# The first expert's output layer in float32, the output weights split during the second expert

## The chip, the cores and the metric

The kernel runs on one core of a Trainium2 chip. The metric is the device time of one launch in microseconds (us); lower is better.

## What is computed

Three layers follow each other: banded attention, a mixture of eight experts in which each token goes to one expert with at most 288 tokens each, and a gated unit. The reference, cut:

```python
B, H, S, D = 4, 8, 576, 64            # attention: a window of 128 keys, a slope per head
attn_out = softmax(scale * q @ k.T + bias, masked) @ v
x = attn_out.transpose(0, 2, 1, 3).reshape(2304, 512)

logits = x @ w_gate                   # 2304 tokens, 8 experts, cap = 288
for idx in np.argsort(-logits.flatten()):      # best pair first
    tok, e = idx // 8, idx % 8
    if assigned[tok] < 0 and counts[e] < cap:
        assigned[tok] = e; counts[e] += 1
x[mask] = np.maximum(x[mask] @ w1[e], 0) @ w2[e]          # per expert, 512 -> 1024 -> 512

g, val = x @ m2_gate, x @ m2_val      # 512 -> 1536, all tokens
out = (g / (1 + exp(-g)) * val) @ m2_out                  # 1536 -> 512
```

## The kernel before

**Stages.** The attention runs first, until about 135 us. Then eight experts follow, one after the other. For each, a routing finds which expert fills up next and the list of its tokens; the tokens are gathered from memory (`xg`), turned on TensorE into `X` with tokens as columns, and taken through all that is left: the first expert layer (8 products, tile `P` used as hidden rows), the second (4 products, `O`), the gate and value layer of the gated unit (12 pairs of products with the weights `GV`), and the output layer with the weights `WO`, whose rows are scattered to the output.

**Precision.** TensorE works on 16-bit pairs: a value is split into a high and a low half, and a product takes three passes (`layer`, L1066). ScalarE makes the high half, VectorE the low one. The first expert alone (`first`, L1103) has its two expert layers in float32 (`layer32`, L1074), so that its weights need no split.

**The gated unit's weights** come as 64-bit integers in 36 chunks, 24 for `GV` and 12 for `WO`, and are turned into float32 on the chip (`glu_weights`, L307). Per chunk VectorE does `shift` (L319, into `cvu`), `join` (L323, into `cvt`), `carry` (L331) and `low` (L346); ScalarE does the lower word (`cvr`) and the high half, both through L293. Most of this runs beside the first expert.

**The first expert's output layer** (`results`, L1177) has two row groups of 128 tokens, c0 and c1, of 12 steps of the inner sum each. For this expert alone they are taken in the order of the weights' arrival: four steps of c0, four of c1, and so on. The other 32 tokens are gathered into `PR` for a later expert. What feeds the layer is `z` (L1146, silu times value), its high half (L1150, ScalarE) and its low half (L1153, VectorE).

**What sets the order.** `Plan` (L120) orders all work before anything runs: each step has an engine, an estimated length and a due time, and a greedy pass takes steps by due time and estimated start. Each engine then runs its own list strictly in order, with waits between engines. `RINGS` gives the number of buffers of each tile, `ROUTE` the due times of the routings relative to the expert's. The second expert's routing (`route`, L717) is a chain of small steps that goes back and forth between VectorE and TensorE while the first expert computes: it ends with the expert's number (`eid`, L813), the choice (`sg`, L818 to L820), places (L840 to L864), a one-hot array (`oc`, L867), 18 small products that list the tokens (L872) and the list itself (`idx`, L877 to L880). Only then can the gather (L1017, GpSimd) start. The expert's weights are loaded through SyncE (L970) into `stw`, three buffers, once `eid` is known, and split by ScalarE (L973) and VectorE (L977) into `WE`.

Of the kernel before, what the change touches and what calls it, by code (L numbers as in the profile page):

```python
# [31 lines left out]
    "stg": 3, "cvt": 4, "cvr": 2, "cvu": 1,  # L32
# [10 lines left out]
ROUTE = ((20, 66), (-5, 30))  # L43
WA = 7
TA, TN = (12, 22), (1.5, 2.5)
GD = (14, 50)
LATE = 1.6
# [72 lines left out]
class Plan:  # L120
# [41 lines left out]
    def ported(self, t, engine):  # L162

        return engine == "Pool" or (engine == "DVE" and t["port"])
# [23 lines left out]
    def run(self, fit, need=None):  # L188
# [5 lines left out]
        while left:  # L194
# [10 lines left out]
            for e, c in by.items():  # L205
# [3 lines left out]
                fits = [x for x in c if x[2] + x[3] <= first[2] + fit]  # L209
# [46 lines left out]
def body(ctx, tc, a, out):  # L256
# [46 lines left out]
    WO = []  # L303
    stage = ctx.enter_context(tc.tile_pool(name="stage", bufs=RINGS["stg"]))
    cv = ctx.enter_context(tc.tile_pool(name="cv", bufs=1))

    def glu_weights(c, due):  # L307
# [9 lines left out]
        def shift(e):  # L317
            v["u"] = cv.tile([128, 512], I32, name="cvu", bufs=RINGS["cvu"])
            nc.vector.tensor_scalar(v["u"], v["f"][:, :, 1], 3, 0x3FFFFFF8, op0=OP.logical_shift_left, op1=OP.bitwise_and)  # L319

        def join(e):
            v["t"] = cv.tile([128, 512], I32, name="cvt", bufs=RINGS["cvt"])
            nc.vector.scalar_tensor_tensor(v["t"], v["f"][:, :, 1], -0x40000000, v["u"], op0=OP.bitwise_and,  # L323
                                           op1=OP.bitwise_or)
# [4 lines left out]

        def carry(e):  # L330
            nc.vector.tensor_add(v["t"], v["t"], v["r"])  # L331

        def parts():
            if c < 24:
                return [GV[:, c % 2, m, c // 2] for m in range(2)]
            d, k = divmod(c - 24, 3)
            return [WO[0][:, m, 4 * k:4 * k + 4, d * 128:d * 128 + 128] for m in range(2)]

        def flat(t):
            return t if c < 24 else t.rearrange("p (k c) -> p k c", k=4)  # L340

        def high(e):
            copy_scaled("ACT", parts()[0], flat(v["t"].bitcast(F32)), SG)

        def low(e):
            nc.vector.scalar_tensor_tensor(parts()[1], flat(v["t"].bitcast(F32)), SG, parts()[0], op0=OP.mult, op1=OP.subtract)  # L346

        add("DMA", dma(2 ** 19), due, fetch, w=[("stg", c)], late=LATE)
        add("DVE", dve(512, 2), due, shift, r=[("stg", c)], w=[("cvu", c)], port=True)
        add("DVE", dve(512), due, join, r=[("stg", c), ("cvu", c)], w=[("cvt", c)], port=True)  # L350
        add("ACT", act(512), due, lower, r=[("stg", c)], w=[("cvr", c)])
        add("DVE", 0.66, due, carry, r=[("cvr", c)], w=[("cvt", c)], port=True)
# [589 lines left out]

    WO.append(big.tile([128, 2, 12, DM], F16, name="WO"))

# [62 lines left out]
    def tokens(k, u):  # L1007
# [13 lines left out]
        for c in range(3):  # L1021
            add("Pool", 1.03, u - ta, lambda e, c=c: fetch(e, c),
                r=[("idx", k)] + [("x_dram", b, kt) for b in range(B) for kt in range(5)], w=[("xg", k, c)])
# [58 lines left out]
    def expert(k, u):  # L1082
# [47 lines left out]
        for f in range(12):  # L1130
            v = {}
            for m in range(2):
# [10 lines left out]
                else:  # L1143
# [4 lines left out]

                    def high(e, f=f, v=v):
                        nc.scalar.activation(P()[:, 0, f], v["z"], AF.Copy)  # L1150
# [3 lines left out]

                    add("DVE", dve(CAP), u, value, r=[key, ("tt", (k, f))], w=[("z", (k, f))])
# [7 lines left out]
        def gather_rest(e):  # L1163
            if ("PR", g) not in T:
                T["PR", g] = wk.tile([128, 2, 12, 128], F16, name="PR", bufs=RINGS["PR"])
            if e == "ACT":
                nc.scalar.activation(T["PR", g][:, :, :, r], P()[:, :, :, 256:CAP], AF.Copy)
            else:
                nc.vector.tensor_copy(T["PR", g][:, :, :, r], P()[:, :, :, 256:CAP])

        add({"ACT": act(768), "DVE": dve(768)}, None, u, gather_rest, r=[y for f in range(12) for y in both("P", (k, "P"), f)],
            w=[("PR", g, k % 4)])
        pieces = {3: (0, 1, 2), 7: (0, 2, 1)}.get(k, (0, 1))
        for c in pieces:
            v = {}

            def results(e, a, c=c):  # L1177
# [3 lines left out]
                for kk in range(4 * a, 4 * a + 4):  # L1181
# [101 lines left out]
```

## Time and profile before

| | |
|---|---|
| Median of 3 runs | 874.05 us (873.32 to 874.25) |
| The profiled execution | 875.06 us |
| Its span, first to last instruction | 873.3 us |
| TensorE busy | 819.2 us, 94% of the span |
| VectorE busy | 507.9 us, 58% |
| ScalarE busy | 343.5 us, 39% |
| Share of the chain that ended last | TensorE 73%, VectorE 10%, waiting for nothing shown 10%, DMA 3% |

A share of the span is a mean over stages with different limits; the page's rows in 40 slices show VectorE at 80 to 90% of each slice from the second to the twelfth (22 to 262 us) and mostly well below that afterwards, while TensorE is full nearly everywhere except in slices 7 and 8 (131 to 175 us) and slices 12 and 13 (240 to 284 us). A stage is read from the timelines: which engine waits, and for whom. A wait stands in square brackets behind the row that ended it.

### The profile page before, as it was taken

Reading aid. Unit: us, or ns where it says so; the run is one execution under the profiler, and the core shown is the slowest. Engines: PE = TensorE matmul, PEld = TensorE weight load, DVE = VectorE, ACT = ScalarE, POOL = GpSimd, SP = SyncE. Lnnn points to the kernel's source line nnn. Section 1 sums busy time; section 2 is a strip of 40 time slices with the busy share of each in tenths; the row PEclk is TensorE's granted clock in tenths of the full one; section 3 lists DMA queues with packets and bytes.
Section 4 is the critical chain, followed back from the end, with each engine's and each line's share of the span. In section 5 each row is a group of like instructions: output and inputs, shape, how many; then the busy total and the mean of one; then the engine's idle time right before and its main releaser. Section 6 shows DMA issues by size and latency. Waiting matters only on the chain.

```text
span 873.3 us, 16974 instructions
## 1 busy us (share of the span) xinstructions
PE 819.2 (94%) x6666; PEld 589.5 (68%) x6666; DVE 507.9 (58%) x1585; ACT 343.5 (39%) x774; POOL 136.5 (16%) x195
## 2 busy tenths in 40 slices
PE   7999994699965999999999999999999999999997
PEld 6887883377732678577757764777577667757763
DVE  3888889889995648445833671367337735312220
ACT  5788882255543314312521341135113434212220
POOL 5586761100002001000100011001000020000001
PEclk9999996599986999999999999999999999999999
DMA  8798523754536004201400240024002532000000
GB/s 274 300 322 300 182 68 91 271 196 162 157 112 220 25 1 151 85 10 66 153 28 2 81 141 36 3 73 149 25 1 100 170 116 81 2 13 13 2 1 36
DMA packets 32064, 92.05 MB, mean 105 GB/s; under 512 B 3952, under 2 KB 10480, under 8 KB 31216
## 3 DMA queue, kind: packets, MB, share of 16 engines
q1 hardware_dynamic: 29008, 81.53, 27.8%
q0 software_dynamic: 2976, 9.44, 3.2%
q8 instruction: 52, 0.85, 0.4%
q14 instruction: 28, 0.23, 0.1%
HBM read 81.52 MB, written 9.44 MB: 104 GB/s over the span
## 4 chain that ended last, share of the span: by engine, by line
PE 73%; issue 10%; DVE 10%; DMA 3%; ACT 2%; POOL 1%; SPq 0%; POOLq 0%; DVEq 0%; ACTq 0%
PE mm L1071 45%; PE mm L1183 13%; PE mm L1077 3%; PE s L535 3%; PE mm L1040 2%; PE o L595 2%; PE t L555 2%; DVE cvt L331 1%; DVE cvt L323 1%; DMA x_dram<-xr 1%; PE rp L872 1%; PE rp L765 1%; DVE tl L570 1%; DVE sc L543 1%; DVE WO L346 1%
## 5 line engine op out<-in xcount | busy, mean ns | idle before, releaser
L1071 PE MATMUL mm<-O,GV 128*128 128x288 f16 x2304 | 292.0, 286 | 0.0
L1071 PEld LDWEIGHTS <-GV 128*128 128x128 f16 x2304 | 220.8, 98 | 55.7
L1071 PEld LDWEIGHTS <-WE 128*128 128x128 f16 x1344 | 128.1, 98 | 34.7 <-issue 1.6
L1183 PE MATMUL mm<-WO,P 128*128 128x512 f16 x576 | 131.2, 385 | 0.0
L1183 PEld LDWEIGHTS <-P 128*128 128x128 f16 x576 | 55.5, 99 | 65.4 <-issue 3.3
L1150 ACT ACTIVATE P<-z 128x288 f16<-128x288 f32 x96 | 42.3, 441 | 120.1 <-DVE z L1146 118.3
L1071 PE MATMUL mm<-X,WE 128*128 128x288 f16 x672 | 89.2, 290 | 0.0
L1071 PE MATMUL mm<-P,WE 128*128 128x288 f16 x672 | 86.1, 286 | 0.0
L977 DVE SCALAR_TENSOR_TENSOR WE<-stw,WE 128x512 f16<-128x512 f32 x112 | 74.0, 684 | 4.6 <-ACT WE L973 4.4
L1192 POOL DMA_INDIRECT out_dram<-R,idx x16 | 16.0, 999 | 381.9 <-ACT R L1188 362.3
L1146 DVE SCALAR_TENSOR_TENSOR z<-mm,t 128x288 f32<-128x288 f32 x96 | 43.6, 454 | 48.7 <-PE mm L1071 48.1
L1017 POOL DMA_INDIRECT xg<-x_dram,idx x24 | 24.9, 1037 | 290.7 <-issue 204.6
L973 ACT ACTIVATE WE<-stw 128x1024 f16<-128x1024 f32 x56 | 58.3, 1051 | 18.0 <-DMA stw<-in_w_dram 17.9
L535 PE MATMUL s<-kt,qb 128*128 128x192 f32 (+2 forms) x288 | 58.2, 336 | 4.6 <-DMA kt<-in_kT_dram 4.6
L1153 DVE TENSOR_TENSOR P<-z,P 128x288 f16<-128x288 f32 x96 | 43.9, 457 | 28.8 <-ACT P L1150 26.6
L549 ACT ACTIVATE pb<-sc,mx 128x192 f32<-128x192 f32 (+2 forms) x144 | 56.0, 431 | 10.6 <-DVE mx L543 10.4
L1140 ACT ACTIVATE t<-mm 128x288 f32<-128x288 f32 x96 | 39.2, 409 | 47.7 <-PE mm L1071 43.7
L535 PEld LDWEIGHTS s<-kt,qb 128*128 128x128 f32 x288 | 46.6, 203 | 6.7 <-DMA qb<-in_qB_dram 4.0
L1000 DVE SCALAR_TENSOR_TENSOR P<-mm,P 128x288 f16<-128x288 f32 x56 | 25.5, 455 | 43.1 <-ACT P L995 41.4
L543 DVE CUSTOM_DVE_ANT_0 sc<-s,bias 128x192 f32<-128x192 f32 (+2 forms) x144 | 41.7, 330 | 13.4 <-PE s L535 11.4
L995 ACT ACTIVATE P<-mm 128x288 f16<-128x288 f32 x56 | 23.0, 410 | 63.2 <-PE mm L1071 62.9
L555 PE MATMUL t<-cst,pb 128*128 128x128 f32 x256 | 43.1, 286 | 2.3 <-ACT pb L549 1.9
(141 smaller groups left out, 1002.0 us busy)
## 6 DMA issues: line engine op xcount, KB each, us to landing
stw<-in_w_dram SPq DMA_DIRECT2D x56, 512.0 KB, 3.7
stg<-in_glu_dram SPq DMA_DIRECT2D x36, 512.0 KB, 3.7
qb<-in_qB_dram SPq DMA_DIRECT2D x3, 2304.0 KB, 13.3
x_dram<-xr SPq DMA_DIRECT2D x16, 256.0 KB, 4.1
WE<-in_w_dram SPq DMA_DIRECT2D x8, 512.0 KB, 5.2
kt<-in_kT_dram SPq DMA_DIRECT2D x3, 1152.0 KB, 8.6
vf<-in_vN_dram SPq DMA_DIRECT2D x8, 256.0 KB, 4.4
vt<-in_vT_dram SPq DMA_DIRECT2D x4, 512.0 KB, 7.8
```

The lines of the kernel that those rows point to most:

```text
L535: nc.tensor.matmul(v["s"][:, par, c:], QB[b % 2][:, hp * 9 + i], KT[b % 2][:, hp, (i - 2) * 64 + c:(i + 1) * 64], start=True, stop=True)
L543: nc.vector.tensor_tensor_reduce(out=v["sc"][:, par, c:], in0=v["s"][:, par, c:], in1=bias[:, hp, c:], scale=-0.125, scalar=3.0e38, op0=OP ...
L549: nc.scalar.activation(PB[n % NPB][:, par, 64 * par + c:64 * par + W], v["sc"][:, par, c:], AF.Exp, bias=v["mx"][:, par:par + 1], scale=-1.0)
L555: nc.tensor.transpose(v["t"][:, j, :, par, :], PB[n % NPB][:, par, j * 128:j * 128 + 128], ident)
L973: nc.scalar.activation(WE[:, c, 0], v["f"], AF.Copy, scale=sc)
L977: nc.vector.scalar_tensor_tensor(WE[:, c, 1, at], f[:, at], sc, WE[:, c, 0, at], op0=OP.mult, op1=OP.subtract)
L1071: nc.tensor.matmul(p[:, :at.stop - at.start], w(i, k), x[:, j, k, at], start=(m == 0), stop=(m == 3 * nk - 1))
L1140: nc.scalar.activation(v["t"], T["mm", k, ("gv", f, 0)][:, :CAP], AF.Silu, scale=1.0 / (SO * SG))
L1146: nc.vector.scalar_tensor_tensor(v["z"], T["mm", k, ("gv", f, 1)][:, :CAP], SPR / (SO * SG), v["t"], op0=OP.mult, op1=OP.mult)
L1150: nc.scalar.activation(P()[:, 0, f], v["z"], AF.Copy)
L1153: nc.vector.tensor_sub(P()[:, 1, f], v["z"], P()[:, 0, f])
L1183: nc.tensor.matmul(T["mm", k, "y", c], x[:, i, kk, at], WO[0][:, j, kk, :], start=(kk == 0 and i == j), stop=(kk == 11 and i == 1))
```

## The change

**Weights.** A `WO` chunk ends with `carry`, which now writes float32 straight into `WO`'s place (`WOF`, a float32 view). Its high and low halves are made later by a new function, `split_output_weights`, due during the second expert: per step of the inner sum ScalarE copies the float32 row to a `stg` buffer and writes the high half, VectorE the low half: 24 ScalarE and 12 VectorE instructions.

**The first expert.** `single_value` writes silu times value as float32 into `P`, in place of `z` and its two halves. The output layer takes these and the float32 weights: 24 float32 products in place of 72 16-bit ones. The 32 left tokens are split by one ScalarE and one VectorE instruction (`rest_high`, `rest_low`).

**Chunks.** `shift` writes into the chunk's own `cvt`; `cvu` is gone and `cvt` has 5 buffers. The planner has a new number, `NEAR`: in its last pass it may let VectorE take a step that can start earlier though another is due up to 1.6 us before it. The first `ROUTE` pair moves by 8 us. GpSimd's DMA issues no longer hold the planner's port between VectorE and GpSimd.

```diff
-    "stg": 3, "cvt": 4, "cvr": 2, "cvu": 1,
+    "stg": 3, "cvt": 5, "cvr": 2,
-ROUTE = ((20, 66), (-5, 30))
+ROUTE = ((12, 58), (-5, 30))
+WS = 90
+NEAR = 1.6
...
-        return engine == "Pool" or (engine == "DVE" and t["port"])
+        return t["port"] if engine == "DVE" else engine == "Pool" and t["port"] is not None
...
-                fits = [x for x in c if x[2] + x[3] <= first[2] + fit]
+                fits = [x for x in c if x[2] + x[3] <= first[2] + fit or (e == "DVE" and x[2] + 0.1 < first[2] and x[0] < first[0] + near)]
...
         def carry(e):
-            nc.vector.tensor_add(v["t"], v["t"], v["r"])
+            if c < 24:
+                nc.vector.tensor_add(v["t"], v["t"], v["r"])
+            else:
+                dst = WOF(slice(4 * a4, 4 * a4 + 4))[:, :, d * 128:d * 128 + 128].bitcast(I32)
+                t, r = (x.rearrange("p (k c) -> p k c", k=4) for x in (v["t"], v["r"]))
+                nc.vector.tensor_add(dst, t, r)
...
+                    if first:
+                        add("DVE", dve(CAP), u, single_value, r=[key, ("tt", (k, f))], w=both("P", (k, "P"), f))
+                        continue
...
+                    if first:
+                        nc.tensor.matmul(T["mm", k, "y", c], single(P, 12)()[:, kk, at], WOF(slice(kk, kk + 1))[:, 0, :],
+                                         start=(kk == 0), stop=(kk == 11))
+                        continue
...
+    def split_output_weights(due):
+        for kk in range(12):
...
+            def copy(e, kk=kk, v=v):
+                v["t"] = stage.tile([128, 512, 2], I32, name="stg").rearrange("p a b -> p (a b)").bitcast(F32)[:, :512]
+                nc.scalar.activation(v["t"], WOF(slice(kk, kk + 1))[:, 0], AF.Copy)
...
+            raw, when = [("WOr", kk, d) for d in range(4)], due + 3 * kk
+            add("ACT", act(512), when, copy, w=[("stg", 100 + kk), *raw])
+            add("ACT", act(512), when, high, r=[("stg", 100 + kk)], w=[("WO", kk, 0)])
+            add("DVE", dve(512), when, low, r=[("stg", 100 + kk), ("WO", kk, 0)], w=[("WO", kk, 1)], port=True)
...
+        if k == 0:
+            split_output_weights(u + WS)
-    plan.run(FIT[1])
+    plan.run(FIT[1], near=NEAR)
```

**How the order moves.** Lines of the changed kernel lie some 10 higher from L341 on: its L878 is the old L867, its L988 the old L977.

VectorE, late in the first expert's gate and value layer, before:

```order
L346 SCALAR_TENSOR_TENSOR WO<-cvt,WO 128x4x128
L323 SCALAR_TENSOR_TENSOR cvt<-stg,cvu 128x512
L331 ISA cvt<-cvt,cvr 128x1024
L1153 TENSOR_TENSOR P<-z,P 128x288
L319 TENSOR_SCALAR cvu<-stg 128x512
```

and after:

```order
L1161 SCALAR_TENSOR_TENSOR P<-mm,t 128x288
L329 SCALAR_TENSOR_TENSOR cvt<-stg,cvt 128x512
L326 TENSOR_SCALAR cvt<-stg 128x512
L345 ISA WO<-cvt,cvr 128x4x256
L780 CAST c_4150<-rp 128x3x32
```

The `low` step of `WO` and the low half of `P` are gone, and a shift of the next chunk stands between a join and its carry.

VectorE, the end of the second expert's routing, before:

```order
L858 TENSOR_TENSOR po<-pos,aa 128x18
L864 SCALAR_TENSOR_TENSOR rh<-pos,cst 128x18 x3
L867 TENSOR_TENSOR oc<-k_slot,po 128x2304
L977 SCALAR_TENSOR_TENSOR WE<-stw,WE 128x512 x3
L877 TENSOR_SCALAR p_4507<-rp 128x2
L878 TENSOR_SCALAR idx_2985<-rp 128x1
```

and after:

```order
L869 TENSOR_TENSOR po<-pos,aa 128x18
L1161 SCALAR_TENSOR_TENSOR P<-mm,t 128x288
L875 SCALAR_TENSOR_TENSOR rh<-pos,cst 128x18 x3
L988 SCALAR_TENSOR_TENSOR WE<-stw,WE 128x512
L878 TENSOR_TENSOR oc<-k_slot,po 128x2304
L988 SCALAR_TENSOR_TENSOR WE<-stw,WE 128x512 x4
L888 TENSOR_SCALAR p_4352<-rp 128x2
```

One low half of the second expert's weights now stands ahead of the one-hot array and four, not three, between it and the list. Further up, between `eid` and `oc`, two shifts, two joins and two carries have come in.

TensorE, from the end of the gate and value layer: before, all 48 products of the first two thirds of the output layer came first, then the last routing steps and `sg`, then this:

```order
L834 LDWEIGHTS k_ones
L834 MATMUL rp<-sg,k_ones 128x36
L835 LDWEIGHTS k_tri
L835 MATMUL rp<-sg,k_tri 128x36
L1183 LDWEIGHTS P
L1183 MATMUL mm<-WO,P 128x512
```

with 24 such pairs of L1183 ahead of the list's 18 products (L872). After:

```order
L845 LDWEIGHTS k_ones
L845 MATMUL rp<-sg,k_ones 128x36
L846 LDWEIGHTS k_tri
L846 MATMUL rp<-sg,k_tri 128x36
L1214 MATMUL mm<-WO,P 128x512 x8
L883 LDWEIGHTS oc
L883 MATMUL rp<-rh,oc 128x3
```

The routing's choice is counted ahead of the whole output layer, the list comes after 8 of the 24 float32 products, and 12 more stand between it and the turning of `X`; the last 4 follow the turning. From the middle of the second expert on TensorE's list is the same but for small routing steps.

## Rows read from the trace of the kernel before

**Rows 1.** busy time of each engine, granted clock and DMA by stretch (PE, PEld, DVE, ACT, POOL)
```profile
175.00:243.88 68.88, 68.53 (x453) 51.66 (x452) 62.42 (x130) 39.30 (x77) 0.00 (x0) 1.00 0.53 172
254.44:261.86 7.42, 0.72 (x12) 0.54 (x13) 7.15 (x22) 1.80 (x4) 0.00 (x0) 0.67 0.00 0
269.69:284.00 14.31, 5.00 (x31) 3.08 (x30) 6.85 (x21) 3.94 (x6) 4.49 (x5) 0.65 0.65 212
```

**Rows 2.** TensorE's timeline: start, length, instruction, idle time before it
```profile
243.88 10.56 PE L1183 MATMUL mm<-WO,P 128*128 128x512 f16 x48
...
261.80 0.19 PE L834 MATMUL rp<-sg,k_ones 128*128 128x36 f16 x1 [2.88 <-DVE sg L820]
...
261.86 8.00 PE L1183 MATMUL mm<-WO,P 128*128 128x512 f16 x24
269.69 1.22 PE L872 MATMUL rp<-rh,oc 128*128 128x3 f16 x18
...
281.18 2.89 PE L1040 MATMUL mm<-cst,xg 32*128 32x32 f32 x10 [0.60 <-DMA xg<-x_dram,idx]
...
289.33 1.64 PE L1071 MATMUL mm<-X,WE 128*128 128x288 f16 x12
```

**Rows 3.** VectorE's timeline, the second expert's routing up to its token list
```profile
260.68 0.15 DVE L813 TENSOR_SCALAR eid<-cd 128x1 int32<-128x1 f32 x1
...
262.07 0.22 DVE L840 TENSOR_TENSOR_SCAN inc<-cst,rp 128x36 f32<-128x36 f32 x1
...
264.54 1.35 DVE L867 TENSOR_TENSOR oc<-k_slot,po 128x2304 f16<-128x2304 f16 x1
266.34 1.29 DVE L977 SCALAR_TENSOR_TENSOR WE<-stw,WE 128x512 f16<-128x512 f32 x2 [0.46 <-ACT WE L973]
...
271.15 0.16 DVE L879 TENSOR_TENSOR idx<-p,rp 128x2 int32<-128x2 f32 x1
```

**Rows 4.** the third of the second expert's gathers, and all gathers' landing times
```profile
274.70 1.38 POOL L1017 DMA_INDIRECT xg<-x_dram,idx  x1 [0.30 <-issue]
...
DMA to landing us min/median/max: 4.0/5.5/6.4
```

**Rows 5.** groups of instructions by line, 175 to 262 us
```profile
L346 DVE SCALAR_TENSOR_TENSOR WO<-cvt,WO 128x512 f16<-128x512 f32 x12 | 8.3, 692 | 1.1 <-ACT WO L293 0.8
...
L1077 PEld LDWEIGHTS mm<-P,WE 128*128 128x128 f32 x64 | 11.9, 190 | 3.2 <-issue 0.2
```

**Rows 6.** the chain that ended last: start, length, what, count
```profile
177.60 11.84 PE mm L1077 x48
...
226.52 1.57 PE mm L1071 x12
228.26 1.58 PE mm L1071 x12
...
720.21 2.02 PE mm L1040 x12
...
769.38 15.55 PE mm L1183 x72
```

**Rows 7.** VectorE's timeline inside the first expert's gate and value layer
```profile
207.80 0.67 DVE L323 SCALAR_TENSOR_TENSOR cvt<-stg,cvu 128x512 int32<-128x512 int32 x1
208.50 0.69 DVE L331 CUSTOM_DVE_ANT_0 cvt<-cvt,cvr 128x1024 uint16<-128x1024 uint16 x1
209.12 0.43 DVE L319 TENSOR_SCALAR cvu<-stg 128x512 int32<-128x512 int32 x1
209.45 0.17 DVE L794 TENSOR_REDUCE dg<-rp 128x1 int32<-128x8 f32 x1
...
211.32 0.45 DVE L1153 TENSOR_TENSOR P<-z,P 128x288 f16<-128x288 f32 x1
211.69 0.68 DVE L331 CUSTOM_DVE_ANT_0 cvt<-cvt,cvr 128x1024 uint16<-128x1024 uint16 x1
```

**Rows 8.** busy time by stretch, start of the second expert (columns as Rows 1)
```profile
280.00:300.00 20.00, 19.29 (x133) 12.65 (x134) 14.16 (x32) 7.76 (x15) 0.00 (x0) 0.81 0.18 61
```

More of the change, by code (lines that the diff above doesn't have):

```diff
@@ L186, in start, with run @@
         return s
-    def run(self, fit, need=None):
+    def run(self, fit, need=None, near=0.0):
         todo = [t for t in self.todo if t["done"] is None]
@@ L303, in body, with WOF @@
     WO = []
+    def WOF(kk):
+        return WO[0][:, kk].rearrange("p k m c -> p k (m c)").bitcast(F32)
     stage = ctx.enter_context(tc.tile_pool(name="stage", bufs=RINGS["stg"]))
@@ L1022, in tokens @@
             add("Pool", 1.03, u - ta, lambda e, c=c: fetch(e, c),
-                r=[("idx", k)] + [("x_dram", b, kt) for b in range(B) for kt in range(5)], w=[("xg", k, c)])
+                r=[("idx", k)] + [("x_dram", b, kt) for b in range(B) for kt in range(5)], w=[("xg", k, c)], port=None)
             add("DMA", 0.55, u - ta, lambda e: None, w=[("xg", k, c)], late=LATE)
@@ L1187, in rows @@
                 v["R"] = wk.tile([128, DM], F32, name="R", bufs=RINGS["R"])
-                nc.scalar.activation(v["R"], T["mm", k, "y", c], AF.Copy, scale=1.0 / (SPR * SO2))
+                nc.scalar.activation(v["R"], T["mm", k, "y", c], AF.Copy, scale=1.0 / SPR if first else 1.0 / (SPR * SO2))
             def store(e, c=c, v=v):
@@ L1205, in expert, with high, low @@
                     [("PR", g, y) for y in range(4)]
-                add("PE", 12 * pe(DM), u, lambda e, a=a, x=x: results(e, a, x),
-                    r=[z for d in range(4) for z in both("GV", 24 + 3 * d + a)] + src, w=[("mm", (k, "y", x)), ("in order",)])
-                u += 12 * pe(DM)
+                us = 4 * pe(DM, 4) if first else 12 * pe(DM)
+                add("PE", us, u, lambda e, a=a, x=x: results(e, a, x),
+                    r=[("WOr", kk, d) if first else ("WO", kk, d) for kk in range(4 * a, 4 * a + 4) for d in range(4 if first else 2)]
+                    + src, w=[("mm", (k, "y", x)), ("in order",)])
+                u += us
             when = u + (0.2 if k else 0)
             add("ACT", act(512, True), when, rows, r=[("mm", (k, "y", c))], w=[("R", (k, c))])
-            add("Pool", 1.2, when, store, r=[("R", (k, c))] + ([("idx", k)] if c < 2 else [("idx", y) for y in range(4 * g, 4 * g + 4)]), late=LATE)
+            add("Pool", 1.2, when, store, r=[("R", (k, c))] + ([("idx", k)] if c < 2 else [("idx", y) for y in range(4 * g, 4 * g + 4)]), late=LATE, port=None)
+    def split_output_weights(due):
+        for kk in range(12):
+            v = {}
+            def copy(e, kk=kk, v=v):
+                v["t"] = stage.tile([128, 512, 2], I32, name="stg").rearrange("p a b -> p (a b)").bitcast(F32)[:, :512]
+                nc.scalar.activation(v["t"], WOF(slice(kk, kk + 1))[:, 0], AF.Copy)
+            def high(e, kk=kk, v=v):
+                copy_scaled("ACT", WO[0][:, kk, 0], v["t"], SG)
+            def low(e, kk=kk, v=v):
+                nc.vector.scalar_tensor_tensor(WO[0][:, kk, 1], v["t"], SG, WO[0][:, kk, 0], op0=OP.mult, op1=OP.subtract)
+            raw, when = [("WOr", kk, d) for d in range(4)], due + 3 * kk
+            add("ACT", act(512), when, copy, w=[("stg", 100 + kk), *raw])
+            add("ACT", act(512), when, high, r=[("stg", 100 + kk)], w=[("WO", kk, 0)])
+            add("DVE", dve(512), when, low, r=[("stg", 100 + kk), ("WO", kk, 0)], w=[("WO", kk, 1)], port=True)
     for c in range(24, 36):
```

53 lines of the change are left out of this document (32 added, 21 removed).

## The prediction

> **What bounds the kernel now.** I read the stretches first, then TensorE's and VectorE's timelines in the one where TensorE is not full. From 175 to 243.88 us TensorE is busy 68.53 of 68.88 us at a granted clock of 1.00, the 2.4 GHz level [rows 1]; from the second expert's third product on it is full again. What lies between is the gap that the change aims at. The output layer's first 48 products run from 243.88 [rows 2], and then TensorE has nothing: from 254.44 to 261.86 it is busy 0.72 us, VectorE 7.15 of 7.42 [rows 1]. VectorE is still turning weight chunks and runs the second expert's routing between them, so that `eid` comes at 260.68 and the one-hot array at 264.54 [rows 3]; TensorE's count of the choice waited 2.88 us for `sg` [rows 2]. Then all is in series: the last 24 products, the list from 269.69, `idx` at 271.15, the gathers, and the turning of the last `X` pieces from 281.18, which waited for the gather [rows 2, 3]. The clock falls in the gap: 0.67 and 0.65 as means [rows 1], between its 1.2 and 2.4 GHz levels, after TensorE had run dry at 254.44. I use 243.88, the end of the gate and value layer, and 289.33, the start of the second expert's third product [rows 2], as marks: 45.45 us. From there on TensorE's list is nearly the same in both kernels, so what these marks lose or gain, the end should too.
>
> **What is taken from VectorE.** One-chunk instructions cost their pitch, start to start. A carry followed by an unrelated shift has 209.12 - 208.50 = 0.62 us; I take 0.62 for join, carry and low alike. A shift has 209.45 - 209.12 = 0.33, a low half of `P` 211.69 - 211.32 = 0.37 [rows 7]. A carry right behind its own join starts 208.50 - 207.80 = 0.70 us after it, 0.08 more. Up to `eid` the order drops 13 lows (12 of `WO` and one that is now done earlier) and 11 low halves of `P`: 13 x 0.62 + 11 x 0.37 = 12.1 us. It has 3 carries, 2 joins, 3 shifts and one silu product fewer, which are done earlier or later: 5 x 0.62 + 3 x 0.33 + 0.37 = 4.5. Counted up to the one-hot array, a step stands right behind the one that it reads 13 times less often: 13 x 0.08 = 1.0. Sum 17.6 us, if VectorE's other waits stay: `eid` at 260.68 - 17.6 = 243.1. This is where the 8 us of `ROUTE` are paid from; the move alone would give nothing, since VectorE had no room.
>
> After `eid`, before's path to the one-hot array took 264.54 - 260.68 = 3.86 us [rows 3]. The order adds two shifts, two joins, two carries and one weight half: 2 x 0.33 + 5 x 0.62 = 3.8. The array starts at 243.1 + 3.86 + 3.8 = 250.7 and takes 1.34 (to 265.88, where 0.46 us of idle time before 266.34 begins [rows 3]). Four weight halves follow, 2.5, then `idx`, which before was complete 0.40 after the list (269.69 + 1.22 to 271.15 + 0.16 [rows 2, 3]): 254.9. ScalarE's 24 fewer halves in this stretch are off the path, as it was busy only 39.30 of 68.88 us [rows 1].
>
> **What TensorE does now.** A 16-bit product of 512 columns has a pitch of 15.55 / 72 = 0.216 us [rows 6], and a float32 product is four passes, 0.864. The trace has no float32 product of 512 columns. It has them with 288: 48 records in 11.84 us, two records each, 0.493 per product; scaled by columns, 0.493 x 512 / 288 = 0.877. I take 0.866, nearer to the first. The 24 products then cost 20.8 us against 15.6 before, **5.2 us more work for TensorE**, which has to be paid out of the gap.
>
> From the end of the gate and value layer (t = 0): the count of the choice 0.06 (261.80 to 261.86); 8 products 6.93; the list 1.22 [rows 2]; 12 products 10.39. That makes 18.6. Now the layer ends later than before: one more routing group stands in it, three small steps at up to 0.17 each, which is 228.26 - 226.52 - 1.57 [rows 6], some 0.45 together. And at the end of the attention VectorE has a carry and a shift where a join stood: 0.62 + 0.33 - 0.70 = 0.25 more ahead of the first routing. So t = 0 lies at 243.88 + 0.7 = 244.58, and `idx` at t = 10.3. `sg` comes some 1.1 us after `eid`, at 244.2, just ahead of it.
>
> **The gather.** From `idx` (end 271.31) to the last piece (281.18) it took 9.87 us [rows 2, 3], of which 281.18 - 274.70 = 6.48 are the last piece's, against 4.0 to 6.4 from issue to landing over all [rows 4]. I take 9.87 again, since weights are loading beside it in both: `X` can be turned from t = 20.2. TensorE is there at 18.6, so it **waits 1.6 us** for a gather that before it waited for in full. Then the turning 2.02, the row at full clock [rows 6]; three routing steps at 0.17; the last 4 products 3.46; two products of 1.57: 9.1. The third product starts at t = 29.4, allowing 0.1 for the step from the gather. With the 0.7 from above, 30.1 us from the old mark.
>
> **The sum.** 45.45 - 30.1 = **15.35 us off**. The profiled execution took 875.06 us, of which 873.3 is the span; 875.06 - 15.35 = 859.7. The median of the runs lies 1.0 below that execution, so 858.7; I say **858.6**. Bounds: a gather that is wholly hidden gives 1.6 more, and 0.7 more if neither delay ahead of t = 0 shows: 856.4. A last piece 2.5 us later, the whole spread of landings over again, gives 861.1.
>
> **What is moved and costed at nothing.** The split needs 24 ScalarE and 12 VectorE instructions in the second expert. VectorE's are 12 x 0.62 = 7.4 us; ScalarE's, priced by the length of a 512-column half on VectorE, 0.692 [rows 5], some 16.6. From 280 to 300 ScalarE is busy 7.76 of 20 us and VectorE 14.16 [rows 8], and the halves are read only in the second expert's output layer, some 65 us after its start: the cover is TensorE's own products of that expert. If the cover were gone, the 7.4 us of VectorE would stand before that layer. What is late next: `X`'s halves on ScalarE stand behind seven weight pieces and five copies of `WO`, the last of which needs the output layer's second third. They have until t = 26.0 (the 4 products and two counts after the turning), against 22.3 for the turned `X`; one weight piece more or less is hidden. SyncE's queue changes little: the chunk loads stay ahead of `stw`. On GpSimd the gathers now stand ahead of the first scatter, which nobody waits for.
>
> **A rule weighed.** The float32 weight loads take 190 ns each [rows 5], two per product, and are hidden: a product of 288 columns takes 0.493 us, no more than its four passes would at the pitch of 16-bit ones, 1.57 / 12 each [rows 6], and not 0.38 more. The Trainium skill (TensorE: Matmul & The Clock Gate, Part 3, The mechanism) says that a weight load overlaps products in flight only where the two use different row groups. Here all use all 128 rows, so by that rule the loads would add to the products; the trace speaks against it for this form, and the third rival is what it would give.
>
> **The rivals.**
> 1. *The gather takes the place of the wait.* More weight pieces (six, not four) are loaded before `X`, and the gathers share the DMA engines with them: share 0.65 in that stretch already [rows 1]. With 2.5 us more the time is 861.1. If the idle time also lets the clock fall as it did after 254.44, the turning, four products and two 16-bit products take twice as long, 2.02 + 3.46 + 3.14 = 8.6 us more: 869.7. For it: a wait of 1.6 us is already in my sum. Against: TensorE is busy for 18 us right before.
> 2. *VectorE stays the bound.* It now waits more for TensorE's products and ScalarE's silu, so that less than 17.6 us come back. Each us lost there is lost at the end. With 4 us, 862.6. Against: TensorE gives its products no later than before.
> 3. *Weight loads are not hidden* behind 512-column passes: 48 loads of 0.19, 9.1 us, 867.7. Against: they hide behind shorter ones.
> 4. *Slower: the float32 products run at the lower clock.* All 24 at 1.2 GHz take twice 20.8, so 20.8 more: 879.4. It decides from 15.35 / 24 = 0.64 us more per product, 1.51 in all. For it: this very stretch had 0.65 to 0.67. Against: float32 products ran at 1.00 from 177 us on, and the fall came after TensorE had run dry.
> 5. *It does not do what it says*: the routing comes no earlier, since the list still waits for `oc`. Then only the 5.2 us show, some 879. The order of VectorE speaks against it.
>
> **How the numbers follow.** Forecast (856.4 to 861.1) 0.72; the first rival 0.12, the second 0.07, the third 0.04, the fourth and fifth together 0.03, and 0.02 for a small change either way. The range of 8 in 10 takes in the first two rivals up to a clock that falls in part, and 0.2 below the forecast's own end: 856.2 to 864.5. Faster by over 0.2% (1.7 us, about what a measurement of this kernel can tell from no change) 0.95, within it 0.02, slower 0.03.
>
> **What would show it.** Right: TensorE's 8, list and 12 follow the gate and value layer with gaps under 1 us, then one gap of 1 to 3 us on `xg`; float32 records of 0.43 us; clock 1.00 through the stage; the third product at about 274; the split's VectorE halves done before the second expert's gate and value layer. Wrong: TensorE waiting for `sg` or `oc` (the second rival), a gap over 3 us on the gather, record pitches well over 0.44, or TensorE waiting on ScalarE in the second expert.

## The result

| | before | changed |
|---|---|---|
| Median | 873.68 us (873.07 to 874.25) | 861.89 us (860.11 to 862.41) |
| Span of the profiled execution | 873.3 us | 860.3 us |
| From the end of the gate and value layer to the third product of the second expert | 45.45 us | 27.89 us |
| End of the gate and value layer | 243.88 | 248.68 |

The ratio is 0.9862, with a 95% interval of 0.9844 to 0.9879. The kernel became faster, inside the range of 856.2 to 864.5 and 3.3 us slower than forecast. The gap in TensorE's work closed further than the prediction had it, but the changed kernel comes to that gap 4.8 us later.

### The profile after

Most lines of the changed kernel lie 11 higher; L1214 is the first expert's output layer. Busy time by stretch, columns as in [rows 1], whose last line they answer to:

```profile
256.69:267.15 10.46, 10.46 (x28) 4.67 (x28) 10.31 (x26) 6.77 (x9) 3.38 (x4) 1.00 0.81 269
268.00:284.00 16.00, 16.00 (x114) 10.30 (x114) 13.83 (x32) 13.99 (x28) 2.55 (x3) 1.00 0.10 38
```

TensorE is busy for the whole of both stretches, at a granted clock of 1.00, the 2.4 GHz level, where [rows 1] had 0.65. VectorE is still nearly full, but nobody waits for it. TensorE's timeline from the end of the gate and value layer (answers to [rows 2]; start, length, instruction, and in brackets the idle time before it):

```profile
248.68 0.18 PE L845 MATMUL rp<-sg,k_ones 128*128 128x36 f16 x1
...
248.74 7.11 PE L1214 MATMUL mm<-WO,P 128*128 128x512 f32 x16
255.69 1.22 PE L883 MATMUL rp<-rh,oc 128*128 128x3 f16 x18
256.77 10.55 PE L1214 MATMUL mm<-WO,P 128*128 128x512 f32 x24
267.15 2.18 PE L1051 MATMUL mm<-cst,xg 128*128 128x128 f32 x12
...
269.54 3.70 PE L1214 MATMUL mm<-WO,P 128*128 128x512 f32 x8
...
273.36 1.64 PE L1082 MATMUL mm<-X,WE 128*128 128x288 f16 x12
...
275.05 4.58 PE L1082 MATMUL mm<-X,WE 128*128 128x288 f16 x36
```

No row has a bracket, nor has one of those left out: the 2.88 us for `sg` in [rows 2] are gone, and so is the wait for the gather. The row at 275.05 holds three products of 12; the first takes to 276.57, where the third product of the expert begins. VectorE's routing steps (answers to [rows 3]):

```profile
245.57 0.15 DVE L824 TENSOR_SCALAR eid<-cd 128x1 int32<-128x1 f32 x1
...
246.01 0.46 DVE L1161 SCALAR_TENSOR_TENSOR P<-mm,t 128x288 f32<-128x288 f32 x1 [0.30 <-PE mm L1082]
...
253.32 1.35 DVE L878 TENSOR_TENSOR oc<-k_slot,po 128x2304 f16<-128x2304 f16 x1
...
257.18 0.16 DVE L890 TENSOR_TENSOR idx<-p,rp 128x2 int32<-128x2 f32 x1
```

`eid` comes 3.1 us ahead of the end of the layer, not 16.8 us behind it, and VectorE now waits for TensorE's product (0.30). The second and third of the second expert's gathers on GpSimd, and from the view of the tile `xg` the time from issue to landing, which the trace has for the second alone (answers to [rows 4]):

```profile
259.37 0.95 POOL L1028 DMA_INDIRECT xg<-x_dram,idx  x1 [0.30 <-issue]
260.63 1.38 POOL L1028 DMA_INDIRECT xg<-x_dram,idx  x1 [0.31 <-issue]
```

```profile
DMA to landing us min/median/max: 4.3/4.3/4.3
```

If the third took as long, the last piece was there at 260.63 + 4.3 = 264.9. TensorE wants it at 267.15 and did not wait.

### Where the 4.8 us ahead of the gap come from

| mark | before | after | later by |
|---|---|---|---|
| first list (L872, L883) | 160.15 | 161.59 | 1.44 |
| first expert's first product | 170.95 | 174.29 | 1.90 more |
| start of the gate and value layer | 206.83 | 210.84 | 0.67 more |
| its end | 243.88 | 248.68 | 0.79 more |

The first of these is made at the end of the attention. VectorE and GpSimd there, in the changed kernel:

```profile
134.33 0.69 DVE L341 CUSTOM_DVE_ANT_0 cvt<-cvt,cvr 128x1024 uint16<-128x1024 uint16 x1
...
134.89 2.11 POOL L298 TENSOR_SCALAR k_slot<-cst 128x2304 f16<-128x2304 f32 x1 [0.48 <-PE o L606]
134.94 2.35 DVE L326 TENSOR_SCALAR cvt<-stg 128x512 int32<-128x512 int32 x1
...
138.46 0.30 DVE L743 TENSOR_REDUCE bst<-logits 128x18 f32<-128x144 f32 x1
```

The shift of a weight chunk that the new order has put here takes 2.35 us; shifts elsewhere take 0.42. It starts 0.05 us after GpSimd began to write the table `k_slot` and ends 0.29 us behind that write. In the kernel before GpSimd wrote the same table a little later and met only small steps. Its timelines there, VectorE's and GpSimd's:

```profile
137.04 0.62 DVE L733 TENSOR_TENSOR w<-logits,bst 128x144 f32<-128x144 f32 x1
137.70 0.31 DVE L737 TENSOR_TENSOR w<-w,cst 128x144 f32<-128x144 f32 x1
```

```profile
135.40 2.11 POOL L296 TENSOR_SCALAR k_slot<-cst 128x2304 f16<-128x2304 f32 x1 [0.48 <-PE o L595]
```

The step at 137.04 began beside the last 0.47 us of that write and took 0.62 us, a like one behind it 0.31.

The second line of the table above is the gather. The landing of the second of its three pieces, before and after, from the view of the tile `xg`:

```profile
DMA to landing us min/median/max: 4.0/4.0/4.0
DMA to landing us min/median/max: 5.8/5.8/5.8
```

Two loads of weight chunks go out in the same time: SyncE issues them at 162.21 and about 166, the gathers at 164.29 to 167.38, so that the second load stands between the gathers. Before, the two loads were issued at 158.45 and about 161.8, both ahead of the first gather at 162.98. SyncE's timeline after, from the issue of the first to that of the second:

```profile
162.21 4.11 SPq L322 DMA_DIRECT2D stg<-in_glu_dram  x2
```

### The profile page after: what moved, and what is told of

It reads as the page before. It is cut to its first block, busy times and chain, and to the rows that moved or that the text cites. A ratio compares the mean times of both kernels' runs of the same rounds, so it can differ in the third digit from the quotient of the medians.

```text
span 860.3 us, 16923 instructions
## 1 busy us (share of the span) xinstructions
PE 818.0 (95%) x6642; PEld 589.5 (69%) x6642; DVE 505.2 (59%) x1574; ACT 345.4 (40%) x774; POOL 137.3 (16%) x195
## 4 chain that ended last, share of the span: by engine, by line
PE 73%; issue 11%; DVE 7%; POOL 3%; DMA 2%; ACT 2%; SPq 1%; POOLq 0%; DVEq 0%; ACTq 0%
PE mm L1082 46%; PE mm L1218 12%; PE mm L1088 4%; PE mm L1214 2%; PE s L546 2%; PE mm L1051 1%; PE o L606 1%; DMA x_dram<-xr 1%; DMA kt<-in_kT_dram 1%; DVE sc L554 1%; PE t L566 1%; PE rp L776 1%; SPq L282 1%; PE rp L883 1%; PE rp L785 1%
## 5 line engine op out<-in xcount | busy, mean ns | idle before, releaser
L1218 PE MATMUL mm<-WO,P 128*128 128x512 f16 x504 | 112.7, 379 | 0.0
L1218 PEld LDWEIGHTS <-P 128*128 128x128 f16 x504 | 48.1, 98 | 55.2
L1165 ACT ACTIVATE P<-z 128x288 f16<-128x288 f32 x84 | 37.1, 441 | 110.5 <-DVE z L1157 110.4
L988 DVE SCALAR_TENSOR_TENSOR WE<-stw,WE 128x512 f16<-128x512 f32 x112 | 74.4, 685 | 3.5 <-ACT WE L984 3.4
L1157 DVE SCALAR_TENSOR_TENSOR z<-mm,t 128x288 f32<-128x288 f32 x84 | 38.2, 455 | 47.9 <-PE mm L1082 46.9
L1168 DVE TENSOR_TENSOR P<-z,P 128x288 f16<-128x288 f32 x84 | 38.5, 458 | 23.4 <-ACT P L1165 22.4
L1006 ACT ACTIVATE O<-mm 128x288 f16<-128x288 f32 x32 | 13.2, 411 | 78.8 <-PE mm L1082 75.5
```

The lines of the kernel that those rows point to most:

```text
L988: nc.vector.scalar_tensor_tensor(WE[:, c, 1, at], f[:, at], sc, WE[:, c, 0, at], op0=OP.mult, op1=OP.subtract)
L1006: nc.scalar.activation(dst()[0], tile()[:, :CAP], AF.Relu if relu else AF.Copy, scale=scale)
L1157: nc.vector.scalar_tensor_tensor(v["z"], T["mm", k, ("gv", f, 1)][:, :CAP], SPR / (SO * SG), v["t"], op0=OP.mult, op1=OP.mult)
L1168: nc.vector.tensor_sub(P()[:, 1, f], v["z"], P()[:, 0, f])
L1218: nc.tensor.matmul(T["mm", k, "y", c], x[:, i, kk, at], WO[0][:, kk, j, :], start=(kk == 0 and i == j), stop=(kk == 11 and i == 1))
```

## The experiments

The theory: the gain in the gap is what the prediction said, and what is missing is lost ahead of it, at these two places. The rivals: the shift waited for its own chunk; the gather is slow by itself; and, for the gain, that only one part of the change brings it. Ratios are to the kernel before, run on the same chip; a run's first product is that of the first expert.

| kernel | median us | ratio, 95% interval |
|---|---|---|
| changed, second time | 861.29 | 0.9855 (0.9841 to 0.9869) |
| k_slot on ScalarE | 860.97 | 0.9854 (0.9833 to 0.9875) |
| loads held | 859.19 | 0.9840 (0.9821 to 0.9860) |
| both | 855.53 | 0.9792 (0.9774 to 0.9811) |
| both, second time | 856.25 | 0.9806 (0.9781 to 0.9830) |
| both, no interleaving | 856.55 | 0.9817 (0.9796 to 0.9837) |
| no interleaving | 860.80 | 0.9854 (0.9834 to 0.9874) |
| routing back by 8 us | 870.88 | 0.9978 (0.9967 to 0.9990) |
| before, routing 8 us earlier | 865.47 | 0.9905 (0.9890 to 0.9919) |
| split made twice as long | 860.98 | 0.9858 (0.9844 to 0.9872) |

### k_slot on ScalarE

```diff
-        e, k_slot, cst[:, at["slot"], None].to_broadcast([128, 128, NT]), 1.0), [("cst",)], [("cst", "slot")])
+        "ACT", k_slot, cst[:, at["slot"], None].to_broadcast([128, 128, NT]), 1.0), [("cst",)], [("cst", "slot")])
```

> The changed kernel, but the table k_slot is written by ScalarE, not by GpSimd; order of all other instructions is unchanged. In the changed kernel VectorE's shift at 134.94 took 2.35 us, beside GpSimd's 2.11 us for k_slot at 134.89; a shift elsewhere takes 0.42. Theory: GpSimd's write holds VectorE. Then the shift takes 0.4 us, the first routing's first step (138.46) starts at about 136.4 to 136.8, the list of the first routing (161.59) some 1.8 us earlier, and the time falls from 861.9 to about 860.1 (859.7 to 860.6). Rival: the shift waited for its own chunk, whose load was issued at 133.20; then it still ends at about 137.3 and the time stays at 861.9. Second rival: the routing comes 1.8 us earlier but the gather, behind the same loads, does not; then the list moves and the first expert's first product (174.29) does not, time 861.9.

VectorE's timeline of this kernel:

```profile
134.97 0.69 DVE L341 CUSTOM_DVE_ANT_0 cvt<-cvt,cvr 128x1024 uint16<-128x1024 uint16 x1
135.58 0.42 DVE L326 TENSOR_SCALAR cvt<-stg 128x512 int32<-128x512 int32 x1
...
137.17 0.30 DVE L743 TENSOR_REDUCE bst<-logits 128x18 f32<-128x144 f32 x1
```

The shift takes 0.42, so it was GpSimd that held it, and the rival with the chunk's own load is out: the load was in no way changed. From the carry (L341) to the routing's first step (L743) it is 2.20 us, 1.93 less than the 4.13 above. The attention ended 0.64 later in this execution, so list and first product come only 1.29 and 1.06 us earlier. In the median hardly anything shows of the 1.8 us expected: 0.9854 against 0.9855 and 0.9862 for the changed kernel. The second rival is thus half right: what the routing gained met a gather as slow as in the changed kernel, 6.0 us.

### Loads held behind the gather

```diff
-HOLD = range(0, 0)
+HOLD = range(9, 11)
...
-        tokens(k, u)
+        tokens(k, u); [plan.follow(loads[c], plan.writer["xg", 0, 2]) for c in HOLD if k == 0]
```

`follow` makes a step wait for what another step waits for, here a load for what the gather waits for. A chunk in `HOLD` is also loaded behind a small GpSimd write into its buffer.

> The changed kernel, but the two chunk loads that SyncE issued at 162.2 and 166 us stand behind the first expert's three gather issues (each waits for a small GpSimd step behind them). Theory: these two loads, 1 MB, shared the DMA engines with the first gather, which took 5.8 us from issue to landing, against 4.0 in the kernel before. Then it lands in 4.0 to 4.5 us, the turning ends some 1.5 us earlier, the first product of the first expert starts at about 172.8 rather than 174.29, and the time falls to about 860.4. Rival: the gather waits for the first four loads of the expert's own weights or is as slow by itself; then 174.29 stays, and the time is 861.9. Second rival: the chunks come too late and VectorE or TensorE waits for them in the gate and value layer: up to 3 us slower, 862 to 865.

The edit did half of this. SyncE's chunk loads in this kernel, from the issue of the first to that of the second:

```profile
161.70 6.64 SPq L322 DMA_DIRECT2D stg<-in_glu_dram  x2
```

One load still goes out at 161.70, ahead of the gathers. The next goes out at about 168, behind the third gather (166.86), where it stood between them in the changed kernel. So one load was taken out of the gather's way and not two; it is the same in the kernels below that hold loads.

The gather of this kernel, from the view of the tile `xg`, and TensorE's turning (which ends at 172.16 with the first product):

```profile
DMA to landing us min/median/max: 4.1/4.1/4.1
```

```profile
168.28 0.63 PE L1051 MATMUL mm<-cst,xg 128*128 128x128 f32 x4 [1.54 <-issue]
...
172.16 4.12 PE L1088 MATMUL mm<-X,WE 128*128 128x288 f32 x8 [0.23 <-ACT X L1064]
```

The landing is what the theory said, with one load moved: 4.1 us, the first product 11.08 us behind the list instead of 12.70, and the median about 0.2% under the changed kernel's. TensorE did not wait for a later chunk. One thing weakens it: with a load between the gathers the landing took 4.5, 4.5, 5.3, 5.8, 6.0 and 6.6 us in six profiled executions (four kernels of this study beside the changed one twice), and in the two at 4.5 the first product came 10.67 and 10.88 us behind the list, no later than here. Held back, as here and in the kernels below, the load left it at 3.5, 3.5, 3.8 and 4.1. So a load between the gathers makes them slower and uneven, and the 1.6 us stand for a wide spread. The interval of the ratio overlaps that of the changed kernel; it is the trace that carries this.

### Both

> Both edits together: k_slot written by ScalarE and the two chunk loads behind the gather. If both delays are real and lie one behind the other on the path (the routing ends before the gather starts), the gains add: 861.9 - 1.8 - 1.5 = 858.6. If the one only uncovers the other (an earlier gather meets more of the weights' loads), about 860. If neither was the cause, 861.9.

The median fell by some 6 us, more than the two gains together, and the five runs spread from 853.9 to 858.8. The profiled one was the slowest of them, so it was run again.

> The kernel with both edits (k_slot written by ScalarE, the two chunk loads behind the first gather), for a second time. Its five runs spread from 853.9 to 858.8 us, and the profiled one was the slowest of them, so where the rest of its gain lies could not be seen. If the two gains add, as the first run said (ratio 0.9792), its ratio to the kernel before is again 0.977 to 0.981, and a usual execution shows the first product of the first expert at about 168 to 169 us, against 174.29. If it was luck, the ratio is 0.983 to 0.985, about the gain of the held loads alone.

Second time: 0.9806, not luck, though the first product comes at 169.74, later than expected. This execution (span 853.1) shows where the surplus lies. TensorE's first products of the first expert, then its clock from 172 to 176 us:

```profile
167.45 1.29 PE L1051 MATMUL mm<-cst,xg 128*128 128x128 f32 x8 [1.67 <-issue]
...
169.74 2.21 PE L1088 MATMUL mm<-X,WE 128*128 128x288 f32 x8 [0.36 <-ACT X L1064]
...
172.07 2.21 PE L1088 MATMUL mm<-X,WE 128*128 128x288 f32 x8
```

```profile
172.00:176.00 4.00, 4.00 (x19) 2.95 (x19) 3.92 (x11) 2.82 (x6) 0.00 (x0) 1.00 0.99 384
```

The changed kernel in the same places, its clock again over 172 to 176 us:

```profile
170.69 1.09 PE L1051 MATMUL mm<-cst,xg 128*128 128x128 f32 x4 [3.47 <-issue]
...
174.29 4.21 PE L1088 MATMUL mm<-X,WE 128*128 128x288 f32 x8 [0.23 <-ACT X L1064]
...
178.68 2.81 PE L1088 MATMUL mm<-X,WE 128*128 128x288 f32 x8
```

```profile
172.00:176.00 4.00, 3.77 (x18) 2.57 (x19) 2.12 (x5) 0.71 (x2) 0.00 (x0) 0.50 0.97 371
```

The first two groups of eight records (two records are one float32 product) take 4.47 us at a clock of 1.00, and 7.14 in the changed kernel, whose clock is at 0.50, the 1.2 GHz level, behind the 3.47 us for which TensorE stood still ahead of the turning. That is 2.7 us more. In this execution the shorter wait thus paid twice. It did not in the first run of this very kernel: TensorE stood still for 0.78, 0.23 and 0.56 us around the pieces of the turning, its clock over 172 to 176 us was 0.50, and the two groups took 7.39 us. With the load alone held they took 6.38. What decides between the two levels here stays open, and it may be what spreads the runs. Part of the surplus lies ahead of these groups: from the list to the first product the two executions of this kernel take 10.32 and 9.70 us, where the changed kernel takes 12.70.

This kernel beats both of the given ones, by 17 us the one before and by some 5 us the changed one.

### No interleaving

```diff
-NEAR = 1.6
+NEAR = 0.0
```

> The changed kernel with the planner's NEAR at 0: joins, carries and lows of two chunks are no longer interleaved on VectorE. The prediction priced the interleaving at 13 x 0.08 = 1.0 us of VectorE's time up to the one-hot array. In the changed kernel VectorE waits for TensorE's products in this layer, and the one-hot array was done 1.0 us ahead of the list. Theory: that slack takes the 1.0 us, and the time stays at 861.9 (861.4 to 862.4). Rival: the interleaving is worth more, since a weight chunk that comes later holds a product of TensorE or the list: 1 to 2 us more, 862.9 to 863.9, with TensorE waiting for GV, WO or oc.

The ratio did not change (0.9854), and in its trace TensorE waits for none of `GV`, `WO` or `oc`. The theory holds: what VectorE saves there has slack behind it.

> Both edits, and the planner's NEAR at 0, so that chunks are no longer interleaved on VectorE. NEAR at 0 alone was no slower (ratio 0.9854). Theory: the interleaving is worth nothing here either: within 1 us of the kernel with both edits. Rival: with the routing 3 us earlier VectorE is the bound again in the gate and value layer, and the 1.0 us that the interleaving saves shows: 1 us or more slower, with TensorE waiting for sg, oc or GV.

The same beside both other edits: 856.55 against 855.53 and 856.25. The intervals don't exclude a loss of 0.4%, so the times alone do not settle it. The traces speak for the theory: TensorE waits for none of `sg`, `oc` or `GV`, and of the 1.7 us between the two profiled executions (spans 854.8 and 853.1) 1.69 are those of the first two groups of eight records, 6.16 and 4.47.

### The routing alone, and everything but the routing

```diff
-ROUTE = ((20, 66), (-5, 30))
+ROUTE = ((12, 58), (-5, 30))
```

This edit in the kernel before:

> The kernel before with only the second expert's routing due 8 us earlier. The prediction said that this alone would give nothing, since VectorE is full: each routing step that comes earlier pushes a step of the weights back, and TensorE then waits for WO's halves instead of the routing: 871 to 875, within 0.2% of the kernel before. Rival: in the new order 24 of the 72 products of the output layer stand behind the turning and 24 between the list and the turning, so that they cover the gather, and the weights' steps fit into what VectorE idles later: then it gains most of what the whole change did, 861 to 866, and the float32 layer is not what the gain comes from.

The rival was right about the time: 865.47 us, 0.9905, two thirds of what the whole change gained. The prediction's "the move alone would give nothing" is wrong. TensorE's timeline of this kernel:

```profile
243.59 2.75 PE L1183 MATMUL mm<-WO,P 128*128 128x512 f16 x12
246.92 0.18 PE L834 MATMUL rp<-sg,k_ones 128*128 128x36 f16 x1 [0.58 <-DVE sg L820]
...
253.71 1.28 PE L872 MATMUL rp<-rh,oc 128*128 128x3 f16 x18 [3.99 <-DVE oc L867]
254.84 7.31 PE L1183 MATMUL mm<-WO,P 128*128 128x512 f16 x24
...
262.96 1.88 PE L1040 MATMUL mm<-cst,xg 32*128 32x32 f32 x10 [0.37 <-DMA xg<-x_dram,idx]
268.45 7.48 PE L1183 MATMUL mm<-WO,P 128*128 128x512 f16 x24 [3.61 <-ACT WO L293]
...
279.08 1.15 PE L1071 MATMUL mm<-X,WE 128*128 128x288 f16 x8
```

VectorE was full, but full of steps that could wait: pushing the weights' steps behind the routing costs TensorE one wait of 3.99 us for `oc` and one of 3.61 for `WO`'s halves, where the routing's lateness had cost far more. The waits sum to 8.55 us, and the two groups of 24 products at a lower clock take 7.31 and 7.48 in place of the 5.2 that 24 take at 0.216 each, 4.4 more. Against that stand the 5.2 us that float32 costs TensorE: 8.55 + 4.4 - 5.2 = 7.7, and from the end of the layer to the third product this kernel does take 279.08 - 243.59 = 35.49, 7.6 more than the changed one. Most of that it has back ahead of the gap: its layer ends 5.1 us earlier than the changed kernel's. Of these 5.1 us 1.9 are not the edit's: the first product comes 1.9 us earlier than even in the kernel before, and up to there the two have the same order on every engine.

The same edit taken back in the changed kernel:

> The changed kernel with the second expert's routing due 8 us later, as in the kernel before; float32 output layer, late split and interleaving stay. In the order the last count of the choice now stands after 12, the list after 16 of the 24 float32 products, and the turning after all of them. Theory (the prediction's: the time that VectorE saves is worth something only through the earlier routing): eid comes some 8 us later than 245.6, the gather's last piece lands some 7 us after the 24 products are done, TensorE waits for it at a falling clock, and the time is 5 to 9 us above the changed kernel, 866 to 870 where that takes 861. Rival: VectorE takes the routing's steps as soon as it has nothing else, so the due time matters little: within 1.5 us of the changed kernel.

9.6 us above the changed kernel of the same set, a little more than the upper end. VectorE's and TensorE's timelines in this kernel:

```profile
248.67 0.15 DVE L788 TENSOR_SCALAR fu<-rp 32x8 bf16<-32x8 f32 x1 [2.31 <-PE rp L785]
252.41 0.17 DVE L817 TENSOR_REDUCE mx<-rp 128x1 f32<-128x8 f32 x1 [3.59 <-PE rp L794]
```

```profile
248.57 3.70 PE L1214 MATMUL mm<-WO,P 128*128 128x512 f32 x8
252.20 0.18 PE L794 MATMUL rp<-fu,k_unit 32*128 32x8 bf16 x1
...
263.93 3.68 PE L1214 MATMUL mm<-WO,P 128*128 128x512 f32 x8
270.81 0.30 PE L1051 MATMUL mm<-cst,xg 128*128 128x128 f32 x1 [3.20 <-DMA xg<-x_dram,idx]
272.98 0.48 PE L1051 MATMUL mm<-cst,xg 128*128 128x128 f32 x1 [1.87 <-DMA xg<-x_dram,idx]
...
277.03 3.06 PE L1082 MATMUL mm<-X,WE 128*128 128x288 f16 x12
```

The list stands after 20 of the 24 products, not after 16. The expected wait for the gather is there, 3.20 and 1.87 us, with a product at 3.06 instead of 1.57 behind it. What was not expected: VectorE, now with time to spare, waits for TensorE (2.31 and 3.59 us), because the routing's small products stand behind blocks of four float32 products, 3.7 us each. The routing alone gives 0.95%, all the rest alone 0.22%, both together 1.4%. That is some 0.3% more than the sum, little more than the intervals allow: the rest is worth more with the earlier routing than without it, but the routing does not need the rest for most of its gain.

### The split made twice as long

```diff
+            add("ACT", act(512), when, high, r=[("stg", 100 + kk)], w=[("WO", kk, 0)])
+            add("ACT", act(512), when, high, r=[("stg", 100 + kk)], w=[("WO", kk, 0)])
+            add("DVE", dve(512), when, low, r=[("stg", 100 + kk), ("WO", kk, 0)], w=[("WO", kk, 1)], port=True)
```

> The changed kernel with each step of the output weights' late split made twice more on ScalarE (the high half three times in all) and once more on VectorE: 24 x 0.65 = 15.6 us more of ScalarE's and 12 x 0.62 = 7.4 us more of VectorE's time in the second expert. Theory: the split is hidden under TensorE's products of the second expert, as the prediction said, and has room: within 1 us of the changed kernel. Rival: ScalarE makes the halves of X and P between the split's steps and sets the second expert's pace: up to 15.6 us more, with TensorE waiting for X or P between 270 and 335 us.

860.98 against 861.29 us. Busy time in the second expert, this kernel:

```profile
266.00:333.00 67.00, 66.65 (x551) 48.85 (x552) 53.32 (x140) 44.07 (x85) 5.71 (x7) 1.00 0.22 74
```

and the changed one, from its own start of that expert:

```profile
268.00:335.00 67.00, 66.65 (x553) 49.00 (x553) 45.92 (x128) 30.96 (x61) 5.72 (x7) 1.00 0.22 73
```

ScalarE does 13.1 us more, VectorE 7.4, and TensorE is busy for 66.65 of 67 us in both. The split is hidden and has room.

### The changed kernel again

> The changed kernel itself, for a second time, beside the kernels of this set, so that they can be set against it on the same chip. If it repeats, the ratio to the kernel before lies within 0.9844 to 0.9879, and its stretch from the first product of the first expert to the third product of the second is again 276.57 - 174.29 = 102.3 us, within 0.3; what moves from run to run should lie ahead of that first product.

The ratio repeats. The stretch measures 276.76 - 175.09 = 101.7 us (its row of three products starts at 275.24), 0.6 shorter, outside what was expected: the first two groups of eight records take 6.54 us here and 7.14 in the first execution, so what moves from run to run lies behind the first product too.

## Why the prediction was right, and where it was off

- **The gap.** Predicted were 29.4 us from the end of the layer to the third product, measured 27.9. Eight products took 6.95 us (6.93 predicted), the list's step 1.08, twelve products 10.38 (10.39). The float32 price, scaled from 288 columns, was right: 0.87 us per product. The four terms up to the turning were predicted at 18.6 and took 18.47. The gap is 27.7 to 27.9 us in all nine profiled executions that have both the float32 layer and the earlier routing.
- **The gather's wait, predicted 1.6 us, was 0.** `idx` ended 8.7 us behind the end of the layer, not 10.3. The third gather went out 260.63 - 257.34 = 3.3 us later, and with the 6.48 us that the last piece took before it would have been there at 18.4, just ahead of TensorE's 18.47. So `idx` was the mis-sized term. The landing was priced at the longest of its spread, but that alone would not have removed the wait each time: in the nine executions it took 4.2 to 5.8 us, and 10.3 + 3.3 + 5.8 is still 0.9 us too late.
- **VectorE.** The prediction let VectorE set the time of `eid`, and its 17.6 us were too few. `eid` comes 3.1 to 3.2 us ahead of the end of the layer, where 1.5 were predicted, in all nine executions, though that end lies anywhere from 241.5 to 248.9 us: the routing's steps there follow TensorE's small products, the last of them at 244.16 in the changed kernel. With both edits `eid` comes at 238.35, 22.3 us earlier than in the kernel before. The second rival (VectorE stays the bound) did not come.
- **The delay ahead of the gap, predicted 0.7 us, was 4.8.** This is the step that failed. It counted two instructions at their own lengths, 0.25 us, and three routing steps, 0.45. The price of the first was set by what ran on GpSimd beside it: 1.93 us, shown by moving that work. The kernel before had lost 0.31 beside the same write, so the list comes 1.44 later. The gather's 1.6 to 1.9 us came from a load that the new order had moved between the gathers, shown by holding it, within a wide spread. The clock, which rose later behind it, accounts for the 0.67 of the next row: the first two groups of eight records took 7.14 us (granted clock 0.60 as a mean) against 4.14 + 0.19 + 2.14 = 6.47 before (0.68), by their starts. The last 0.79, where 0.45 was predicted for one more routing group, is that group too, since each small step also breaks a row of products. By starts in the kernel before, 144 products in a row took 17.75 us and 12 took 1.58: 0.1225 a product and 0.11 a row. Three more steps make three more rows, 0.45 + 0.33 = 0.78.
- **The sum.** 15.35 - 4.1 + 1.5 = 12.75, and 289.33 - 276.57 = 12.76 was gained at the marks; the rest of the program takes 583.73 us against 583.97. These marks explain 2.6 of the 3.3 us between forecast and median. Most of the others come from the step to the median: the prediction took 1.0 off the profiled execution, and the changed kernel's median lies only 0.2 below its own (862.10). The measured time lies 0.8 above the forecast's own end, which is also that of the first rival, 861.1, but that rival's mechanism did not occur: no wait for the gather in the second expert, and a clock of 1.00. The range held the time because it had been widened for that wait; the loss lay ahead of the gap, where no rival looked, and in so far it was luck. Of the signs named, the gap of 1 to 3 us on `xg` and the third product at about 274 did not come.
- **The move of the routing alone** was said to give nothing. It gives 0.95%, two thirds of the whole, so the time taken from VectorE was not what paid for most of it. A full engine is no proof that order does not matter; what counts is whether the steps put back are needed soon.
- **Weight loads** are hidden behind the 512-column passes as well. The group of them, 248.6 to 273.2 us (count, then busy time and mean ns):

```profile
L1214 PEld LDWEIGHTS mm<-WO,P 128*128 128x128 f32 x48 | 8.9, 191 | 10.2 <-issue 10.2
```

  Two of 191 ns go with a product, and the 16 records from 248.74 still take 6.95 / 16 = 0.434 us each, no more than two of a product's four passes. By the rule of the Trainium skill weighed in the prediction (TensorE: Matmul & The Clock Gate, Part 3, The mechanism) they would have added 9 us; this trace speaks against it for this form too. The same section of the Trainium skill also lets a load go ahead into a background weight buffer, and with that the rows agree.
- **The split** was rightly costed at nothing, and the fourth and fifth rival did not come.

## What to carry to other kernels

When a change moves work, look at what runs at the new place on the neighbouring engine and in the DMA queues, not only at the moved work's own length: here 1.9 us and some 1.6 us were lost in a place that the change was not about. An engine at 90% may still hold the steps that everybody waits for behind steps that nobody does, so try the order by itself before the arithmetic is changed. And measure the parts alone and together: here 0.95% and 0.22% made 1.4%.

## What was not expected of the hardware

- A step of VectorE of 0.42 us stood for 2.35 us beside a GpSimd write of a 128x2304 table of 2.11 us, and ended 0.29 after it; with the write on ScalarE it took 0.42. The Trainium skill (SBUF — State Buffer, SBUF: two separate sides) says that VectorE, in its two-port modes or with two inputs from SBUF against a GpSimd step that reads SBUF, and GpSimd share one pair of ports, which the one that starts first holds to its end. In which mode the shift ran no run here shows; that it was held to the end agrees with the row, where GpSimd had started 0.05 us earlier, and with the 0.62 for 0.31 of a two-operand step in the kernel before.
- Of three gathers by GpSimd, issued alike, the second took from 4.5 to 6.6 us to land in six executions in which a load of 0.5 MB was issued between them, and 3.5 to 4.1 in six in which none was: four with the load held back and two of the kernel before's order.
- In two executions of one kernel TensorE went through the same first products of an expert at a clock of 1.00 and of 0.50, after standing still for 1.67 us ahead of the turning in the first, and for 0.78, 0.23 and 0.56 us around its pieces in the second: 4.47 against 7.39 us for 16 records, which are eight products.
